# Start of a gated-recurrence and maxout kernel: half masks, GpSimd work moved to VectorE, unit products, a new order of steps

## The chip, the cores and the metric

The kernel runs on one core of a Trainium2 chip. The metric is the device time of one execution in microseconds (us). PE is TensorE (matmuls; PEld its weight loads), DVE is VectorE, ACT is ScalarE, POOL is GpSimd, SP the engine whose queue issues all DMAs here.

## The reference

Two parts, one behind the other. First a gated recurrence ("gateloop") over 4 batches, 8 heads, 768 time steps and head size 48. The gate of each step is a complex number whose size is cut to 0.999; the state is a 48x48 matrix for each head:

```python
mag = np.sqrt(a_re * a_re + a_im * a_im)
scale = np.minimum(mag, 0.999) / (mag + 1e-06)
a_re_n, a_im_n = (a_re * scale, a_im * scale)
for t in range(S):
    new_re = ar * S_re - ai * S_im          # ar, ai: the gate at t, along the rows of the state
    new_im = ar * S_im + ai * S_re
    S_re, S_im = (new_re + outer(k[t], v[t]), new_im)
    y[t] = q[t] @ S_re
```

Then a maxout feed-forward layer over the 3072 tokens, with 384 inputs (8 heads x 48) and 768 hidden units:

```python
h = np.maximum(np.maximum(x @ w1, x @ w2), x @ w3)
out = (h @ w_out).astype(np.float32)
```

The four weight matrices come as 64-bit floats; the rest is 32-bit.

## The kernel before

The recurrence is done in chunks. A group g is 128 time steps of two batches; there are twelve groups (6 along time, 2 pairs of batches). The two blocks of a group, one for each batch, are called x and y; a step's name ends in x or y where it works on one block. Groups 0 and 6 start a sequence.

What is done for a group, by the names that the order uses:

- Loads: `Lr` and `Li` (real and imaginary gate), `Lq`, `Lk`, `Lv`.
- Gates, on 128x768 elements for both blocks (in group 0 on 128x384 for one block, with a 0 or 1 behind the name): `sqr` and `sqi` (squares, ACT), `add` (DVE), `lnL`, `expw`, `expe`, `lne`, `relu` (ACT), `Lnop` (DVE: the tile Ln, minus the logarithm of the gate's size), then the gate's angle: `abs`, `addw`, `lnw`, `expL`, `mulai` (the product ai<-ai,L), `mulw`, `stt`, `sign`, `cpai`, `cpar`, `atan`, `carry` (subtracts the angle carried over from the group before, in one row: ai<-ai,carry), `mulr`, `addi`.
- Angles summed along time: `cs` (PE, product with the triangle matrix `upto`), `t`, `nf`, `af`, `sa`, `sb` (sine and cosine, ACT). `Cd` is a DMA that takes the last rows of nf to the next group as its carry.
- Sums of Ln along time: `sums` (PE, products with the matrices `mid` and `rest`), `En`, `Ek`, `Eq` (ACT), and `F` (PE, products with `cuts`), `f0` to `f3` (ACT).
- `mk`, `mq`, `uk`, `uq` turn k and q by their angles (DVE); `tpk`, `tpq` transpose them (PE, 16 products with `ident` each), `Kc` and `Qc` copy the result out of PSUM (ACT); `Q1` to `Q3`, `QB`, `QG`, `KB`, `kEn` scale them (DVE).
- `A` and `B` are the scores (PE), `g0` to `g3` and `b0`, `b1` copy them out under the masks `maskd` and `masko`; `dk` and `h0` to `h3` make the new state; `y` is the output of the recurrence (PE), copied by the step `x` to the tile xT (so `xx` and `xy` for the blocks).
- Feed-forward: `U` and `u` (products with w1 to w3, in the profile `up`, and their maximum, hT), `O` and `o` (product with w_out, in the profile `op`, and its copy), `D` (store). For group 0 they are done by block: `U20x` is the third part of the hidden units with the first matrix for block x. For later groups, both blocks are done at once.
- Weights: twelve blocks i. `WLi` loads one of 768 KB, and `Wai` to `Wfi` turn it from 64 to 32 bits: a and d on ACT, b, c, e and f on DVE.

The order of the work is written out by hand in two strings. `SCHEDULE` holds the start, word by word as step:group. `CYCLE` is then run for g = 2 to 13 (line 765), with offsets, and skips steps of groups that don't exist. Each engine's instructions are bound to this order: the class `Bound` (lines 120 to 134) makes each instruction follow the one before it on its engine, so that all of them carry line 129 in the profile, and they are told apart by their tiles. SP's queue follows the same order, too; an issue that waits for its buffer holds up all those behind it.

Buffers that matter here: PSUM is one pool of four tiles of two banks (`banks`, line 139), taken in turn; the raw weight blocks lie in parts of the weight tiles that aren't filled yet, in a buffer of Q, or in the two buffers of hT (line 305); the gate tiles L, w and e have one buffer each, ar and ai two.

`ident`, `mid`, `rest`, `upto`, `cuts` and the masks are made on POOL, with memsets on DVE or POOL and selects (`affine_select`, in `keep` and `between`), in `constants_early` (line 206) and `constants_late` (line 233, the step `CL`). `mid`, `rest` and `cuts` have the same content in partitions 0 to 63 and 64 to 127, and `constants_early` makes both halves with a loop over `o`. Besides the masks, POOL does the product `mulai` of the groups from 2 on (line 406) and all carries (line 419).

ACT has its functions in two sets of tables; `activation` (line 147) loads a set when the next function isn't in the present one. Exp and Ln are in one set, Arctan and Sin in the other.

Of the kernel before, what the change touches and what calls it, by code (L numbers as in the profile page):

```python
# [17 lines left out]
OP = mybir.AluOpType  # L18
# [1 line left out]


SCHEDULE = """
Lry:0 sqr1:0 Liy:0 sqi1:0 add1:0 lnL1:0 Lrx:0 Lix:0 sqi0:0 sqr0:0 add0:0 expe1:0 WL0:0 expw1:0 lnL0:0 relu1:0
expw0:0 expe0:0 lne1:0 Lnop1:0 WL1:0 lne0:0 WL2:0 relu0:0 Lnop0:0 Wa0:0 Wd0:0 Wb0:0 Wc0:0 abs1:0 addw1:0 WL3:0
abs0:0 Liy:1 addw0:0 We0:0 Wf0:0 sumsx:0 Eqx:0 Fx:0 f0x:0 Fy:0 lnw1:0 lnw0:0 Wa1:0 Wb1:0 expL0:0 mulai0:0
f3x:0 Wc1:0 mulw0:0 Lqx:0 Wd1:0 We1:0 WL4:0 expL1:0 mulw1:0 Ekx:0 Lrx:1 Wa2:0 sign0:0 stt0:0 Enx:0 f0y:0 Wf1:0
Wb2:0 Wc2:0 cpai0:0 Wd2:0 mulai1:0 We2:0 Wf2:0 f2x:0 cpar0:0 atan0:0 stt1:0 mulr0:0 addi0:0 csx:0 Lkx:0 Wa3:0
Lry:1 Lix:1 atan1:0 sign1:0 Wd3:0 cpai1:0 Lqy:0 tx:0 mqx:0 cpar1:0 WL5:0 Wa4:0 Wb3:0 Wc3:0 We3:0 nfx:0 afx:0
Lvx:0 Wf3:0 mulr1:0 Wb4:0 addi1:0 csy:0 Liy:2 Wc4:0 CL:0 Wd4:0 mkx:0 sax:0 We4:0 sbx:0 ukx:0 f1y:0 uqx:0 f1x:0
tpqx:0 WL6:0 sqr:1 sqi:1 Wf4:0 ty:0 Lky:0 add:1 f2y:0 nfy:0 Qcx:0 Q1x:0 f3y:0 QBx:0 Q2x:0 lnL:1 WL7:0 Wa5:0  # L30
expe:1 Wb5:0 expw:1 Lqy:1 tpkx:0 kEnx:0 Kcx:0 lne:1 relu:1 sumsy:0 QGx:0 Q3x:0 Wc5:0 Lnop:1 Wd5:0 We5:0 Wa6:0
Wb6:0 Ax:0 g0x:0 Wc6:0 abs:1 Eky:0 addw:1 Cdy:0 g1x:0 KBx:0 dkx:0 Cdx:0 mky:0 Eny:0 g2x:0 sign:1 Eqy:0 mqy:0
Wd6:0 We6:0 afy:0 lnw:1 h1x:0 h2x:0 sumsy:1 Eqy:1 mqy:1 expL:1 Wd7:0 Lrx:2 Eny:1 Lry:2 sqr:2 mulw:1 mulai:1
say:0 Wf5:0 sby:0 Wa7:0 g3x:0 stt:1 Wf6:0 cpai:1 uky:0 Bx:0 b1x:0 Wb7:0 h3x:0 Lix:2 Wc7:0 b0x:0 uqy:0 atan:1
carry:1 cpar:1 WL8:0 We7:0 sqi:2 add:2 mulr:1 yx:0 xx:0 Eky:1 Wd8:0 Wf7:0 Lvy:0 addi:1 tpqy:0 Qcy:0 Q2y:0
QGy:0 lnL:2 Q1y:0 Wa8:0 Wb8:0 Q3y:0 U20x:0 U10x:0 u20x:0 u10x:0 tpky:0 Kcy:0 KBy:0 csy:1 expe:2 ty:1 nfy:1
Lky:1 csx:1 expw:2 tx:1 relu:2 kEny:0 Wc8:0 lne:2 U11x:0 WL9:0 Wa9:0 Wd9:0 nfx:1 We8:0 u11x:0 U01x:0 Wf8:0
Wb9:0 Lnop:2 dky:0 h1y:0 h2y:0 U00x:0 Ay:0 g0y:0 u00x:0 sby:1 WL10:0 u01x:0 afy:1 Lkx:1 mky:1 Wc9:0 WL11:0
abs:2 h3y:0 say:1 g1y:0 sign:2 addw:2 lnw:2 U21x:0 u21x:0 g2y:0 We9:0 Cdx:1 Wa10:0 QBy:0 U22x:0 u22x:0 g3y:0
uky:1 expL:2 sumsx:1 Eqx:1 Wf9:0 Enx:1 By:0 b0y:0 b1y:0 Wb10:0 Ekx:1 mulw:2 Fx:1 f1x:1 Lqx:1 mqx:1 Wd10:0  # L40
f3x:1 Wc10:0 f0x:1 mulai:2 stt:2 We10:0 U12x:0 u12x:0 Cdy:1 yy:0 xy:0 Lvy:2 uqy:1 Wf10:0 U02x:0 u02x:0 mkx:1
f2x:1 afx:1 cpai:2 carry:2 atan:2 cpar:2 U20y:0 h0x:1 sax:1 U21y:0 mulr:2 U10y:0 sbx:1 Lkx:2 ukx:1 Lqx:2 Lvx:1
u20y:0 u21y:0 U00y:0 U11y:0 uqx:1 Wa11:0 Wb11:0 U12y:0 u10y:0 u11y:0 Wc11:0 addi:2 tpqx:1 Wd11:0 We11:0 u00y:0
u12y:0 Qcx:1 Q2x:1 QBx:1 tpqy:1 Qcy:1 Lqy:2 U01y:0 u01y:0 Lix:3 csy:2 ty:2 nfy:2 csx:2 tx:2 nfx:2 sbx:2 Wf11:0
Lky:2 QGx:1 U22y:0 tpkx:1 u22y:0 Q1x:1 afx:2 sax:2 Kcx:1 KBx:1 Q3x:1 kEnx:1 tpky:1 U02y:0 Liy:3 u02y:0 Fy:1
f0y:1 f3y:1 f1y:1 f2y:1 Q1y:1 Q2y:1 kEny:1 POx:0 Lrx:3 Kcy:1 sumsx:2 Ekx:2 mkx:2 Enx:2 h0y:1 Eqx:2 Ax:1 g0x:1
Q3y:1 dkx:1 g1x:1 h1x:1 Pox:0 g2x:1 h2x:1 sby:2 g3x:1 h3x:1 afy:2 say:2 Lry:3 sqr:3 Bx:1 QBy:1 b0x:1 sqi:3
ukx:2 POy:0 Ay:1 b1x:1 add:3 g0y:1 g1y:1 lnL:3 KBy:1 Lvx:2 g2y:1 g3y:1 Poy:0 Lvy:1 yx:1 xx:1 PDy:0 Fx:2 f0x:2
dky:1 By:1 sumsy:2 f2x:2 QGy:1 h1y:1 h2y:1 f3x:2 f1x:2 b0y:1 b1y:1 yy:1 expe:3 Eny:2 Eqy:2 xy:1 PDx:0 mqx:2
h3y:1 tpkx:2 Cdx:2 uqx:2 tpqx:2 Eky:2 mky:2 uky:2  # L50
"""
# [12 lines left out]


@with_exitstack
def kernel(
# [15 lines left out]
    P = 128  # L83
# [120 lines left out]
    KB = const.tile([P, 2 * H, 32], FP, name="KB")  # L204

    def constants_early():
        for o in (0, L64):
            halves = mid[o:o + L64].rearrange("p (n u h) -> p n u h", u=2, h=4)
            left, right = halves[:, :, 0], halves[:, :, 1]
            dve.memset(left, -1.0)  # L210
            keep(left, -1, [[-8, 8], [-1, 4]], 1)
            keep(left, 3, [[8, 8], [0, 4]], -1)
            keep(right, -4, [[-8, 8], [0, 4]], 1)
            keep(right, 4, [[8, 8], [1, 4]], -1)
            keep(rest[o:o + L64].rearrange("p (n h) -> p n h", h=8), -4, [[-8, 8], [0, 8]], 1)
        keep(upto, 0, [[1, P]], -1)
        make_identity(nc, ident)
        for o in (0, L64):
            def col(base, n):
                return cuts[o:o + L64, base:base + n]  # L220

            between(col(C8, 4), 7, 11, [[16, 4]], [[16, 4]])
            vw = col(C16, 8).rearrange("p (a v b) -> p a v b", a=2, v=2)
            between(vw[:, :, 0], 3, 19, [[32, 2], [0, 2]], [[32, 2], [8, 2]])
            between(vw[:, :, 1], 15, 19, [[32, 2], [-4, 2]], [[32, 2], [8, 2]])
            vw = col(CB, 6).rearrange("p (a n) -> p a n", a=2)
            between(vw[:, :, 0:2], 3, 7, [[32, 2], [16, 2]], [[32, 2], [16, 2]])
# [137 lines left out]
    def gates(g, cs, name):  # L365
# [37 lines left out]
        elif name == "expL":  # L403
            activation(out=L, in_=L, func=AF.Exp, scale=-1.0)
        elif name == "mulai":
            (pool if g > 1 else dve).tensor_tensor(out=ai, in0=ai, in1=L, op=OP.mult)
        elif name == "mulw":
            dve.tensor_tensor(out=w, in0=w, in1=L, op=OP.mult)
        elif name == "stt":
            dve.scalar_tensor_tensor(out=w, in0=w, scalar=2.0, in1=ai, op0=OP.subtract, op1=OP.mult)  # L410
        elif name == "sign":
            activation(out=ar, in_=ar, func=AF.Sign, bias=tiny)
        elif name == "cpai":
            activation(out=ai, in_=ar, func=AF.Copy, scale=-0.25, bias=0.25)
        elif name == "cpar":
            activation(out=ar, in_=ar, func=AF.Copy, scale=-1.0 / math.pi)
        elif name == "carry":
            if g % NS > 0:
                pool.tensor_tensor(out=ai[0:1], in0=ai[0:1], in1=T["carry", g], op=OP.subtract)
        elif name == "atan":  # L420
            activation(out=w, in_=w, func=AF.Arctan)
        elif name == "mulr":
            dve.tensor_tensor(out=w, in0=w, in1=ar, op=OP.mult)
        else:
            dve.tensor_tensor(out=w, in0=w, in1=ai, op=OP.add)
# [291 lines left out]
    def run(name, g):  # L717

        if g >= NG or g == 0 and name in ("Ox", "ox", "Dx", "Oy", "oy", "Dy"):
            return  # L720
        if name[0] == "P":
            name = name[1:]
        if name == "CL":
# [73 lines left out]
```

## Time and profile before

| what | value |
|---|---|
| three runs, median (lowest to highest) | 645.2 us (644.43 to 646.07) |
| the profiled execution | 646.76 us |
| its span | 645.1 us |
| granted TensorE clock, mean | 0.98 |
| PE, PEld busy | 579.1, 473.3 us |
| DVE, ACT, POOL busy | 475.6, 410.3, 75.2 us |
| POOL products ai<-ai,L: 10, mean | 2.43 us |
| POOL carries ai<-ai,carry: 10, mean | 2.84 us |
| ACT table loads: 30, mean | 1.28 us |
| bytes moved | 39.25 MB |

The page of the profile gives for each engine the time in which it had an instruction under way. The table's rows are sums over the span; how busy an engine was in one stage is read from windows. Two instructions on one engine overlap a little, so the time from start to start of two neighbours is up to 0.1 us under the duration of one. "1.71 <-POOL ai L129" behind an instruction says that its engine stood idle for 1.71 us and that POOL's writing of ai released it.

### The profile page before, as it was taken

What the parts mean: (1) busy time and instruction counts of PE and PEld (TensorE: products, weight loads), DVE (VectorE), ACT (ScalarE), POOL (GpSimd) and SP (SyncE); (2) the same over time, 40 slices, a digit from 0 to 9 for tenths busy, and PEclk for the clock granted to TensorE, in tenths of its full rate; (3) what the DMA queues carried; (4) which work ended last, traced back from release to release, by engine and by line L of the source; (5) the groups of instructions that cost most, each with busy time, mean ns of one, the idle gap of its engine ahead of it and who ended that gap; (6) DMA issues with size and microseconds to landing.
All of it is one profiled execution on the core that took longest, in us unless ns stands there. A gap on an engine that the chain in (4) does not pass through costs nothing.

```text
span 645.1 us, 22666 instructions
## 1 busy us (share of the span) xinstructions
PE 579.1 (90%) x10076; PEld 473.3 (73%) x10076; DVE 475.6 (74%) x680; ACT 410.3 (64%) x676; POOL 75.2 (12%) x91
## 2 busy tenths in 40 slices
PE   1134988998999999999999999999999999999997
PEld 0124877677777777878788788788878778778785
DVE  4799989959778778878668678868859759755111
ACT  7799996777477477486586685774774774530100
POOL 8501040003003002001003003002011011000000
PEclk9997889988999999999999999999999999999999
DMA  9856324342132132132231240250240120000000
GB/s 267 173 136 148 82 73 84 75 87 42 30 68 57 33 67 54 37 66 50 40 74 40 40 85 29 40 100 14 43 97 15 36 56 14 15 14 3 13 13 24
DMA packets 136545, 39.25 MB, mean 61 GB/s; under 512 B 129152, under 2 KB 132224, under 8 KB 136448
## 3 DMA queue, kind: packets, MB, share of 16 engines
q1 hardware_dynamic: 136448, 37.80, 26.8%
q8 instruction: 79, 1.29, 0.9%
q14 instruction: 18, 0.15, 0.1%
HBM read 33.03 MB, written 4.72 MB: 59 GB/s over the span
## 4 chain that ended last, share of the span: by engine, by line
PE 82%; issue 8%; POOL 4%; ACT 2%; DMA 1%; DVE 1%; SPq 1%; POOLq 0%; ACTq 0%; DVEq 0%
PE up L129 42%; PE op L129 15%; PE y L129 6%; PE A L129 4%; PE tp L129 4%; PE dk L129 3%; PE sums L129 2%; PE cs L129 2%; PE B L129 2%; PE F L129 1%; POOL cuts L129 1%; DMA raw<-in_moe_w_dram 1%; POOL ai L129 1%; SPq L129 1%; POOL maskf L129 1%
## 5 line engine op out<-in xcount | busy, mean ns | idle before, releaser
L129 PE MATMUL up<-xT,w 128*128 128x256 f32 (+1 forms) x1404 | 298.3, 370 | 2.2 <-DVE hT L129 1.0
L129 PEld LDWEIGHTS up<-xT,w 128*128 128x128 f32 x1404 | 250.7, 193 | 35.0 <-DVE hT L129 1.2
L129 PE MATMUL op<-wo,hT 128*128 128x384 f32 x288 | 98.8, 494 | 0.0
L129 DVE TENSOR_TENSOR hT<-hT,up 128x768 f32<-128x768 f32 (+1 forms) x56 | 46.8, 836 | 52.7 <-PE up L129 52.7
L129 DVE TENSOR_TENSOR Q<-Q,f 112x512 f32<-112x512 f32 (+2 forms) x72 | 75.9, 1067 | 4.9 <-ACT Q L129 4.2
L129 PEld LDWEIGHTS op<-wo,hT 128*128 128x128 f32 x288 | 53.0, 190 | 33.1
L129 POOL TENSOR_TENSOR ai<-ai,L 128x768 f32<-128x768 f32 x10 | 24.3, 2428 | 389.6 <-ACT L L129 334.4
L129 ACT ACTIVATE f<-F 48x280 f32<-48x280 f32 x96 | 38.1, 398 | 18.5 <-PE F L129 12.9
L129 ACT ACTIVATE t<-cs 128x384 f32<-128x384 f32 x24 | 11.8, 491 | 59.5 <-PE cs L129 59.5
L129 PE MATMUL y<-atm,vb 128*32 128x64 f32 x1152 | 40.6, 228 | 8.4 <-DVE ex L129 8.3
L129 PEld LDWEIGHTS y<-atm,vb 128*32 128x32 f32 x1152 | 33.9, 114 | 17.7 <-issue 17.4
L129 PE MATMUL y<-QG,g 112*32 112x64 f32 x1408 | 39.4, 223 | 0.0
L129 ACT ACT_TABLE_LOAD x30 | 38.5, 1283 | 1.2 <-PEq L781 0.8
L129 ACT COPY ot<-op 128x384 f32<-128x384 f32 x24 | 11.5, 480 | 43.5 <-PE op L129 36.0
L129 DVE SCALAR_TENSOR_TENSOR Ln<-L,e 128x768 f32<-128x768 f32 (+1 forms) x13 | 11.7, 897 | 37.2 <-ACT e L129 36.5
L129 PE MATMUL A<-Q,K 112*32 112x80 f32 x1536 | 32.9, 238 | 5.8 <-DVE Q L129 3.9
L129 POOL TENSOR_TENSOR ai<-ai,carry 1x768 f32<-1x768 f32 x10 | 28.4, 2837 | 70.9 <-ACT ai L129 70.9
L129 PEld LDWEIGHTS A<-Q,K 112*32 112x32 f32 x1536 | 28.5, 112 | 11.0 <-ACT e L129 7.4
L129 PEld LDWEIGHTS y<-QG,g 112*32 112x32 f32 x1408 | 36.1, 112 | 0.0
L129 ACT COPY atm<-B 32x256 f32<-32x256 f32 x48 | 17.3, 361 | 28.5 <-DVE atm L129 25.8
L129 ACT COPY hT<-up 128x768 f32<-128x768 f32 (+1 forms) x28 | 19.8, 708 | 23.1 <-PE up L129 20.7
L129 DVE COPY_PREDICATED atm<-maskd,A 128x512 f32<-128x512 uint8 x24 | 17.6, 734 | 22.0 <-PE A L129 22.0
(96 smaller groups left out, 932.1 us busy)
## 6 DMA issues: line engine op xcount, KB each, us to landing
ar<-in_a_re_dram SPq DMA_DIRECT2D x24, 192.0 KB
ai<-in_a_im_dram SPq DMA_DIRECT2D x24, 192.0 KB
q<-in_q_dram SPq DMA_DIRECT2D x96, 48.0 KB
k<-in_k_dram SPq DMA_DIRECT2D x96, 48.0 KB
vb<-in_v_dram SPq DMA_DIRECT2D x96, 48.0 KB
out_dram<-ot SPq DMA_DIRECT2D x24, 192.0 KB
raw<-in_moe_w_dram SPq DMA_DIRECT2D x5, 768.0 KB
w<-in_moe_w_dram SPq DMA_DIRECT2D x2, 768.0 KB
```

What stands on the lines that cost most here:

```text
L129: ins = f(*a, **kw)
```

## The change

- **Half masks.** `constants_early` makes `mid`, `rest` and `cuts` for partitions 0 to 63 only, and copies each to partitions 64 to 127 on POOL. The order on POOL is now mid and rest, cuts, the memsets of fs, upto, ident, the memsets of vbs; before, the memsets of vbs and fs stood first. `constants_early` is called ahead of the DVE memsets of gs and us. ident is made by two instructions in place of a library call.
- **Products and carries.** `mulai` and `carry` are on DVE for every group.
- **Unit products.** `banks` takes a number from `HOT` for four steps of group 0 and issues that many products of ident with ident (128x128) to the PSUM tile that the step then overwrites: 40 ahead of cs, 23 ahead of tpq, 13 ahead of A, 21 ahead of B, all of block x.
- **Order.** `SCHEDULE` is new, 618 words in place of 472, and reaches one group further: `CYCLE` now starts with g = 3. `CYCLE` has its 143 steps in another order. In it, tables are loaded four times a group; before, twice.

```diff
 def banks(nm, n=None):
     ps = psum.tile([P, 2, 512], FP, tag="ps", name=nm)
+    for i in range(T.pop("hot", 0)):
+        mm(out=ps[:, 0, 0:P], lhsT=ident, rhs=ident, start=True, stop=True)
...
 def constants_early():
-    for o in (0, L64):
-        halves = mid[o:o + L64].rearrange("p (n u h) -> p n u h", u=2, h=4)
...
-    keep(upto, 0, [[1, P]], -1)
-    make_identity(nc, ident)
-    for o in (0, L64):
-        def col(base, n):
-            return cuts[o:o + L64, base:base + n]
...
+    halves = mid[0:L64].rearrange("p (n u h) -> p n u h", u=2, h=4)
...
+    for t in (mid, rest):
+        pool.tensor_copy(out=t[L64:P], in_=t[0:L64])
+
+    def col(base, n):
+        return cuts[0:L64, base:base + n]
...
+    pool.tensor_copy(out=cuts[L64:P], in_=cuts[0:L64])
+    for t in fs:
+        pool.memset(t[L64 // 2:L64], 0.0)
+    keep(upto, 0, [[1, P]], -1)
+    pool.memset(ident, 0.0)
+    pool.affine_select(out=ident, in_=ident, compare_op=OP.not_equal, fill=1.0, base=0, pattern=[[-1, P]],
+                       channel_multiplier=1)
+    for t in vbs:
+        pool.memset(t, 0.0)
...
-    (pool if g > 1 else dve).tensor_tensor(out=ai, in0=ai, in1=L, op=OP.mult)
+    dve.tensor_tensor(out=ai, in0=ai, in1=L, op=OP.mult)
...
-    pool.tensor_tensor(out=ai[0:1], in0=ai[0:1], in1=T["carry", g], op=OP.subtract)
+    dve.tensor_tensor(out=ai[0:1], in0=ai[0:1], in1=T["carry", g], op=OP.subtract)
...
+HOT = {("csx", 0): 40, ("tpqx", 0): 23, ("Ax", 0): 13, ("Bx", 0): 21}
...
+    if (name, g) in HOT:
+        T["hot"] = HOT[name, g]
...
-for g in range(2, NG + 2):
+for g in range(3, NG + 2):
     program(CYCLE, g)
```

The first words of `SCHEDULE`, to the second block's cs:

```diff
-Lry:0 sqr1:0 Liy:0 sqi1:0 add1:0 lnL1:0 Lrx:0 Lix:0 sqi0:0 sqr0:0 add0:0 expe1:0 WL0:0 expw1:0 lnL0:0 relu1:0
-expw0:0 expe0:0 lne1:0 Lnop1:0 WL1:0 lne0:0 WL2:0 relu0:0 Lnop0:0 Wa0:0 Wd0:0 Wb0:0 Wc0:0 abs1:0 addw1:0 WL3:0
-abs0:0 Liy:1 addw0:0 We0:0 Wf0:0 sumsx:0 Eqx:0 Fx:0 f0x:0 Fy:0 lnw1:0 lnw0:0 Wa1:0 Wb1:0 expL0:0 mulai0:0
-f3x:0 Wc1:0 mulw0:0 Lqx:0 Wd1:0 We1:0 WL4:0 expL1:0 mulw1:0 Ekx:0 Lrx:1 Wa2:0 sign0:0 stt0:0 Enx:0 f0y:0 Wf1:0
-Wb2:0 Wc2:0 cpai0:0 Wd2:0 mulai1:0 We2:0 Wf2:0 f2x:0 cpar0:0 atan0:0 stt1:0 mulr0:0 addi0:0 csx:0 Lkx:0 Wa3:0
-Lry:1 Lix:1 atan1:0 sign1:0 Wd3:0 cpai1:0 Lqy:0 tx:0 mqx:0 cpar1:0 WL5:0 Wa4:0 Wb3:0 Wc3:0 We3:0 nfx:0 afx:0
-Lvx:0 Wf3:0 mulr1:0 Wb4:0 addi1:0 csy:0 Liy:2 Wc4:0 CL:0 Wd4:0 mkx:0 sax:0 We4:0 sbx:0 ukx:0 f1y:0 uqx:0 f1x:0
...
+Lrx:0 sqr0:0 Lix:0 sqi0:0 add0:0 WL0:0 lnL0:0 Wa0:0 Wb0:0 Wd0:0 Wc0:0 We0:0 Wf0:0 expe0:0 WL1:0 expw0:0 Wa1:0
+Wb1:0 Wc1:0 relu0:0 lne0:0 Lnop0:0 sumsx:0 Wd1:0 We1:0 WL7:0 Wa7:0 Wb7:0 Wd7:0 Fx:0 Wf1:0 Lry:0 sqr1:0 abs0:0
+f2x:0 addw0:0 Liy:0 sqi1:0 Wc7:0 add1:0 We7:0 WL2:0 sign0:0 Lix:1 Wa2:0 Wb2:0 Lqx:0 WL8:0 Wc2:0 lnL1:0 Lvx:0
+Wd2:0 Wf7:0 lnw0:0 Lqy:0 WL3:0 Lkx:0 expe1:0 expw1:0 lne1:0 We2:0 Wf2:0 relu1:0 Lnop1:0 expL0:0 mulw0:0
+mulai0:0 Wa8:0 Wb8:0 f0x:0 abs1:0 Wd8:0 addw1:0 Wc8:0 stt0:0 Eqx:0 mqx:0 We8:0 Ekx:0 lnw1:0 cpai0:0 expL1:0
+mulw1:0 mkx:0 cpar0:0 mulai1:0 stt1:0 atan0:0 mulr0:0 WL5:0 sign1:0 addi0:0 csx:0 WL6:0 Wf8:0 Lky:0 Lry:1
+Liy:1 atan1:0 cpai1:0 Lvx:1 Wa5:0 Wb5:0 cpar1:0 mulr1:0 CL:0 Lrx:1 WL4:0 Lry:2 tx:0 nfx:0 Wc5:0 Wa6:0 Wb6:0
+afx:0 sbx:0 addi1:0 sax:0 Wc6:0 ukx:0 Wd5:0 We5:0 Wd6:0 We6:0 Enx:0 sqr:1 uqx:0 Wf6:0 f1x:0 tpqx:0 sqi:1 f3x:0
+Wf5:0 tpkx:0 csy:0 add:1 kEnx:0 dkx:0 Qcx:0 Q2x:0 QGx:0 Q1x:0 QBx:0 Kcx:0 Fy:0 lnL:1 KBx:0 Q3x:0 Wa4:0 Wb4:0
...
```

The loop after:

```
CYCLE = """
U00:-1 Kcy:0 Q1x:0 Lry:2 Q2x:0 QBx:0 expe:1 Dy:-2 Q3x:0 Kcx:0 Lix:2 Ax:0 KBx:0 Bx:0 Fy:0 kEny:0 g0x:0 u00:-1
f0y:0 relu:1 Ox:-2 lne:1 g1x:0 g2x:0 g3x:0 b1x:0 Lnop:1 abs:1 addw:1 b0x:0 kEnx:0 f2y:0 f3y:0 f1y:0 Q2y:0
lnw:1 expL:1 U10:-1 mulw:1 u10:-1 mulai:1 ox:-2 sumsx:1 Ekx:1 QGx:0 sign:1 Enx:1 Lkx:1 mkx:1 Eqx:1 Cdx:0 stt:1
dkx:0 Q1y:0 Cdy:0 Lqy:1 atan:1 cpai:1 sumsy:1 U11:-1 h0x:0 h1x:0 Eny:1 h2x:0 Q3y:0 h3x:0 cpar:1 u11:-1 sqr:2
mulr:1 Lqx:1 sqi:2 mqx:1 carry:1 U01:-1 addi:1 Eky:1 Lvy:0 mky:1 KBy:0 Eqy:1 u01:-1 QBy:0 U02:-1 u02:-1 Lrx:3
yx:0 csy:1 xx:0 csx:1 Lvx:1 Ay:0 ty:1 nfy:1 g0y:0 g1y:0 g2y:0 tx:1 afy:1 say:1 nfx:1 sby:1 By:0 g3y:0 U12:-1
b0y:0 add:2 Liy:3 sbx:1 b1y:0 afx:1 mqy:1 sax:1 u12:-1 Fx:1 f1x:1 f2x:1 lnL:2 expw:2 uky:1 dky:0 Oy:-1 h0y:0
oy:-1 Lky:2 QGy:0 f0x:1 h1y:0 h2y:0 f3x:1 Dx:-2 uqx:1 h3y:0 yy:0 tpqx:1 xy:0 uqy:1 tpqy:1 Qcx:1 Qcy:1 ukx:1
tpky:1 tpkx:1
"""
```

## The prediction

> **What bounds the kernel now.** I read the kernel by stages first: busy time of each engine in seven windows (us of the window, then busy us of PE, PEld, DVE, ACT, POOL, granted clock, DMA share, GB/s).
>
> ```profile
> 0.00:16.00 16.00, 1.65 (x18) 1.28 (x18) 7.72 (x28) 11.70 (x21) 14.11 (x48) 1.00 0.97 268
> 16.00:32.00 16.00, 2.34 (x68) 2.04 (x70) 11.55 (x19) 12.63 (x23) 8.40 (x24) 1.00 0.84 175
> 32.00:64.00 32.00, 13.16 (x283) 10.10 (x283) 31.25 (x48) 31.46 (x50) 1.94 (x1) 0.88 0.55 136
> 64.00:113.00 49.00, 44.27 (x714) 40.35 (x704) 47.13 (x71) 41.60 (x65) 7.36 (x3) 0.90 0.35 83
> 113.00:185.00 72.00, 66.69 (x1503) 53.89 (x1501) 59.23 (x85) 48.44 (x84) 4.86 (x2) 0.95 0.29 56
> 185.00:577.00 392.00, 387.81 (x6898) 315.93 (x6893) 300.07 (x411) 258.83 (x426) 38.48 (x15) 1.00 0.23 48
> 577.00:645.00 68.00, 63.13 (x617) 49.70 (x615) 18.62 (x24) 5.67 (x11) 0.00 (x0) 0.99 0.05 16
> ```
>
> PE is busy 579.1 us and idle 66.0. The idle time by window: 28.0 before 32 us, 18.8 to 64, 4.7 to 113, 5.3 to 185, 4.2 to 577, 4.9 in the tail. So from 185 us on PE sets the pace and almost nothing can be won. Ahead of that, from 32 to 113 us, DVE is busy 78.4 of 81 us: the start is bound by DVE's queue. Before 32 us DVE is idle 12.7 of 32 us. What PE waits for:
>
> ```profile
> PE sums L129 <- POOL cuts L129: 12.7, 1, 12.7
> PE cs L129 <- DVE w L129: 11.4, 1, 11.4
> PE y L129 <- DVE ex L129: 8.3, 1, 8.3
> ...
> PE cs L129 <- ACT CS L129: 3.9, 1, 3.9
> PE F L129 <- POOL cuts L129: 3.9, 1, 3.9
> PE A L129 <- DVE Q L129: 3.9, 1, 3.9
> ```
>
> All of these lie before 64 us. The timeline of POOL and DVE shows what the moved products and carries cost (start, duration):
>
> ```profile
> 87.44 5.10 POOL L129 TENSOR_TENSOR ai<-ai,L 128x768 f32<-128x768 f32 x1 [22.99 <-ACT L L129]
> 94.49 1.80 POOL L129 TENSOR_TENSOR ai<-ai,carry 1x768 f32<-1x768 f32 x1 [1.95 <-ACT ai L129]
> ```
> ```profile
> 92.58 0.96 DVE L129 SCALAR_TENSOR_TENSOR w<-w,ai 128x768 f32<-128x768 f32 x1 [1.71 <-POOL ai L129]
> ...
> 94.66 2.46 DVE L129 TENSOR_TENSOR uq<-CS,q 128x768 f32<-128x768 f32 x1
> ```
>
> POOL takes 5.10 us for a product that DVE does in 0.96, DVE waits 1.71 us for it, and a DVE step beside the carry takes 2.46 us where its group's mean is 1.02.
>
> [...] the first eight cs products took 1.55 us, sixteen later ones 1.45.
>
> **The change, part by part.** I price queues by start-to-start times of before: DVE 0.87 us for a 128x768 step, 0.47 for 128x384, ACT 0.75 and 0.41, a table load 1.28. On PE at full clock: an up of 18 matmuls 4.0, op 4.07, y 1.72, A 1.25, and so on for all; over the whole kernel this gives 567 us, so of PE's 579 some 12 is slow clock. Added along each engine's order, in us, before / after:
>
> - ahead of the first cs (group 0, block x): DVE 14.7 / 20.2, ACT 20.5 / 23.0
> - ahead of the first y: DVE 50.0 / 51.3, ACT 55.2 / 53.0, PE 8.4 / 8.7
> - ahead of the first op of group 0: DVE 95.4 / 95.2, ACT 96.6 / 94.8, PE 48.5 / 51.5
> - through the last y of group 2: DVE 141.7 / 149.0, PE 110.6 / 111.7
>
> *Masks.* 21 of the 42 selects on mid, rest and cuts go (0.26 to 0.29 us each), three copies come (a 64x64 cast took 0.23). POOL starts about 1.5 us, since the memset of mid now stands ahead of those of g: five selects and two copies to 3.3, sixteen selects and a copy to about 8.3 (before: 18.2), f 1.06, upto 0.67, ident 0.8, the four vb memsets 2.76, to 13.6. F's 3.9 us wait goes. What is late next is DVE's w for cs, so this alone moves nothing on the end. The v load now waits for vb at 13.6; SP stands behind earlier loads until about then, so I cost it at nothing (if not, the q and k loads behind it slip by a few us).
>
> *Order to the first cs.* The new order does block x first and puts weight blocks 0, 1 and 7 between the gates. A block is one load of 0.79 MB, 2.9 us at the 268 GB/s of the first window, two steps on ACT (0.81, 0.83) and four on DVE (0.47, 0.48, 0.87, 0.87). Loads come in SP's order, at that rate from about 2.2 us: block 0 at 6.6, block 1 at 9.5, block 7 at 12.5, y's two inputs at 13.9, block 2 at 16.9, block 8 at 21 to 23 (q and ai between), k of x at 26 to 28. Walking ACT and DVE beside them, each step at the later of its queue and its input: ln's table ends at 6.7; block 0 is on DVE to 10.8; Ln of x is ready at 12.3 (before: both halves at 12.6); block 1 to 14.7; block 7 to 19.6, with y's inputs ahead of it on DVE; block 2 to 21.4; the second Ln 21.9; x's two products 22.4 and 22.8; block 8 waits for its load, to 26.1; the table for atan 26.3 to 27.6; addi 29.1. With small loads slower than the rate, 30.5. So cs starts near 30 against 31.16, but DVE has by then done 20.2 instead of 14.7: it lags its queue sum by 9 to 10 us instead of 16.4. That is 6.5 us won for DVE, all from its 12.7 idle us before 32.
>
> *From there to the first op.* Before: 112.2 us, so the lag of DVE's sum was 16.8, the same as at cs. After: 95.2 + 9.5 = 104.7 from DVE. But PE has 42.8 us of full-clock work between the first y (51.3 + 9.5 = 60.8) and that op, and lost 8.9 of 49 us in that window before (4.7 idle, 4.2 slow clock). I let it keep half: 60.8 + 42.8 + 5 = 109. PE's lag (time less PE's sum) is then 57.5 against 112.2 - 48.5 = 63.7: 6.2 us won.
>
> *Products and carries.* Ten of each leave POOL (2.43 and 2.84 us); DVE gets 0.87 for each (the 1x768 has the same elements in a row, so the same price; a floor of 0.4 and a ceiling of 0.96). Per group 1.7 us more on DVE, less the stretches seen (1.14 at 152, 1.6 at 158, 1.5 at 94): near nothing. In the loop DVE is 77% busy, so that hides it; in the start the queue sums above have it in. If the cover were gone it is 0.3 us a group.
>
> *Unit products.* 97 of 128x128: twelve up matmuls of that shape took 1.53 us, 0.127 each, twice that cold: 5 to 10 us ahead of cs, 3 to 6 of tpqx, 2 to 3 of A, 3 to 5 of B. Cover: F ends about 15.5 and cs starts at 30; between cs and tpqx DVE has 8.5 us of queue; A and B each have about 6. All hidden; uncovered, the two last would cost up to 4. I give them no gain of their own.
>
> *113 to 185 us.* Before lost 5.3 idle and about 4 slow. In the new order DVE's sum plus 14 (the lag when PE is at 109) leaves it 5 us ahead of PE through group 2's last y (163 against 170), and PE has no cold start; 4.5 of the 9 goes.
>
> *The loop.* Same PE work. ACT gets four table loads a group instead of two: 2.57 us more, at 66% busy. I cost it at nothing. SP: the carry DMAs now stand behind steps that finished long ago (before, SP stood 19.0 us for nf at one); the early ar load for group 2 stands for a buffer that frees about 33 us, with loads of groups 1 and 2 behind it that are not yet due.
>
> Sum: 6.2 + 4.5 = 10.7 us. The profiled execution was 646.8 with a span of 645.1, so about 636 for it; the median of before, 645.2, is 1.6 under it, so 634.5 for the median.
>
> **Rivals.** *Hidden anyway:* PE was already 90% busy from 64 us, so DVE's lead may end in PE's queue. Then only the masks and F count, and 644.5 comes out. Against: DVE waits little and PE's waits to 64 us name DVE. *More:* PE stays warm and the start loses nothing: 4.5 more and 4 of the slow clock, 626. *Slower, by the loop:* A of a group follows one up (4.0) on PE and needs K's copy. On ACT, after the last y, stand xT's copy, two Q copies, a K copy, an exp and the second K copy: 0.48 + 3 x 0.92 + 0.75 + 0.92 [...], about 5.3; PE has four tp (2.1) and the up, 6.1. The margin is 0.85 us. If the extra tables make ACT late by their 2.57, PE waits 1.7 in each of nine loops, 15.5: 645.2 - 10.7 + 15.5 = 650. It decides from 1.2 us a loop on. Against: ACT is a third idle.
>
> **Numbers.** Forecast 0.56 (634.5, own range 629 to 641); more 0.12; hidden 0.15, of which a part is still faster; slower 0.17. A change of 0.3%, 1.9 us, is what a measurement can tell. Faster 0.71, same 0.12, slower 0.17. The range runs from 626 (cs at 27 us, nothing lost later) to 648, which takes in the hidden case and the slower end's first third.
>
> **What would show it.** Right: cs about 30 us with DVE busy over 22 us before it; the first op near 109; PE idle under 61 us and slow clock gone after 64; no DVE step of 384 or 768 over 1.1 us beside POOL; from 185 us on the same idle. Wrong: the first op at 112 or later; a wait of A or cs for ACT that comes back in each group; cs waiting behind unit products.

## The result

After: 643.83 us (median of 12 runs, 640.95 to 646.12). Before, on the same chip: 645.13 us (12 runs, 643.49 to 646.66). Ratio 0.9979, 95% interval 0.9961 to 0.9997: 1.3 us faster, where 10.7 were forecast. The two profiled executions lie at the ends of their groups, 646.76 before and 640.95 after, with granted clocks of 0.980 and 0.989; they show 5.8 us where the medians show 1.3. So moments of single profiles are read below to about 2 us (e1 and e9 below are the same program up to the first op, and their profiles have it at 108.9 and 111.1), and worths from ratios of many runs.

The profile after, by the same stages (columns as before):

```profile
0.00:16.00 16.00, 0.00 (x0) 0.00 (x0) 9.86 (x25) 9.63 (x14) 9.87 (x37) 1.00 0.93 261
16.00:32.00 16.00, 12.45 (x128) 12.01 (x128) 15.41 (x27) 15.24 (x29) 4.34 (x3) 0.97 0.86 223
32.00:64.00 32.00, 24.11 (x370) 22.03 (x370) 27.41 (x43) 28.63 (x47) 6.04 (x13) 0.85 0.63 135
64.00:113.00 49.00, 43.68 (x854) 39.86 (x857) 47.85 (x73) 43.76 (x72) 0.00 (x0) 0.97 0.28 67
113.00:185.00 72.00, 65.75 (x1470) 53.84 (x1459) 61.45 (x92) 50.90 (x83) 0.00 (x0) 1.00 0.33 66
185.00:577.00 392.00, 388.28 (x6899) 315.81 (x6898) 305.18 (x427) 275.88 (x438) 0.00 (x0) 1.00 0.22 47
```

DVE is idle 6.7 us before 32 where it was idle 12.7: fed earlier, as forecast. But from 32 to 64 it is idle 4.6 us where it had been idle 0.75, and from 113 to 185 PE is still idle 6.3 (5.3 before). PE's larger busy time before 64 is unit products, 27 us of it. The waits up to 185 us (total, times, longest):

```profile
PE sums L138 <- DVE Ln L138: 16.4, 1, 16.4
DVE atm L138 <- PE A L138: 4.6, 2, 4.4
PE cs L138 <- DVE w L138: 4.1, 1, 4.1
PE A L138 <- DVE nf L138: 3.9, 1, 3.9
```

F no longer waits for the cuts. New is VectorE's wait for A, 4.4 us. The first Ln came at 15.7 and the first cs at 32.97, not at 12.3 and 30; the first op at 114.0, not at 109. Two rows of the timeline (start, duration) show the first of these:

```profile
8.75 3.85 DVE L138 TENSOR_SCALAR ex<-ex 128x768 f32<-128x768 f32 x2 [2.61 <-ACT ex L138]
...
9.41 2.78 POOL L138 MEMSET vb<- 128x768 f32 x4
```

Two weight steps took 3.85 us beside GpSimd's memsets of vb; the same pair took 1.15 at 14.61: 2.7 us lost, about as long as the four memsets (2.78). With the memsets in the same place other profiles lost less (the pair took 2.48 in e2, 2.54 in e14, 1.70 in e9, 1.17 in e1), and with the memsets first nothing (1.16 in e3). Why such a step takes longer beside memsets on GpSimd no run here shows.

The second failing place:

```profile
50.97 4.80 PE L138 MATMUL A<-ident 128*128 128x128 f32 x26 [3.90 <-DVE nf L138]
...
55.70 1.31 PE L138 MATMUL A<-Q,K 112*32 112x80 f32 x64
...
57.15 0.73 DVE L138 COPY_PREDICATED atm<-maskd,A 128x512 f32<-128x512 uint8 x1 [4.36 <-PE A L138]
```

The 13 unit products ahead of A (two instructions each) write A's PSUM buffer, so they start only when that buffer is free, at 50.97, and A itself starts 4.7 us later. They are in A's way, not in an idle stretch.

### The profile page after: what moved, and what is told of

Its sections match the earlier page's. It is cut to its first block, busy times and chain, and to the rows that moved or that the text cites. A ratio compares the mean times of both kernels' runs of the same rounds, so it can differ in the third digit from the quotient of the medians.

```text
span 639.2 us, 22955 instructions
## 1 busy us (share of the span) xinstructions
PE 592.0 (93%) x10270; PEld 489.2 (77%) x10270; DVE 480.1 (75%) x699; ACT 429.1 (67%) x690; POOL 20.2 (3%) x53
## 4 chain that ended last, share of the span: by engine, by line
PE 85%; DVE 8%; ACT 3%; issue 3%; DMA 1%; SPq 0%; DVEq 0%; ACTq 0%
PE up L138 44%; PE op L138 15%; PE y L138 6%; PE A L138 5%; PE tp L138 4%; PE dk L138 3%; PE sums L138 3%; DVE ex L138 2%; PE cs L138 2%; DVE w L138 2%; PE F L138 2%; PE B L138 2%; DMA w<-in_moe_w_dram 1%; DVE Q L138 1%; ACT CS L138 0%
## 5 line engine op out<-in xcount | busy, mean ns | idle before, releaser
L138 PE MATMUL up<-xT,w 128*128 128x256 f32 (+1 forms) x1404 | 292.5, 366 | 3.3 <-ACT xT L138 2.7
L138 PEld LDWEIGHTS up<-xT,w 128*128 128x128 f32 x1404 | 248.0, 190 | 39.9 <-ACT xT L138 3.2
L138 DVE TENSOR_TENSOR hT<-hT,up 128x768 f32<-128x768 f32 (+1 forms) x56 | 46.6, 834 | 48.6 <-PE up L138 48.5
L138 DVE TENSOR_TENSOR Q<-Q,f 112x512 f32<-112x512 f32 (+2 forms) x72 | 67.7, 951 | 11.3 <-ACT Q L138 9.7
L138 ACT COPY xT<-y 128x384 f32<-128x384 f32 x24 | 11.5, 479 | 65.6 <-PE y L138 65.6
L138 ACT COPY hT<-up 128x768 f32<-128x768 f32 (+1 forms) x28 | 19.8, 708 | 36.1 <-PE up L138 36.1
L138 PEld LDWEIGHTS y<-atm,vb 128*32 128x32 f32 x1152 | 32.4, 111 | 11.6 <-issue 8.2
L138 PE MATMUL y<-atm,vb 128*32 128x64 f32 x1152 | 39.3, 223 | 1.0 <-issue 0.8
L138 PEld LDWEIGHTS y<-QG,g 112*32 112x32 f32 x1408 | 34.9, 110 | 2.0 <-ACT g L138 1.0
L138 DVE COPY_PREDICATED atm<-masko,A 128x256 f32<-128x256 uint8 x72 | 31.2, 433 | 1.6
L138 PE MATMUL sums<-Ln,mid 64*64 64x192 f32 x192 | 14.1, 351 | 16.4 <-DVE Ln L138 16.4
L138 PE MATMUL dk<-vb,uk 64*48 64x48 f32 (+1 forms) x1408 | 24.9, 215 | 3.2 <-issue 1.6
L138 DVE TENSOR_TENSOR QG<-Q,f 112x1024 f32<-112x1024 f32 (+1 forms) x24 | 27.1, 1129 | 0.9 <-PE y L138 0.9
```

What stands on the lines that cost most here:

```text
L138: ins = f(*a, **kw)
```

## The experiments

Every run is compared with before on its own chip. Starts are of the profiled execution (us); "PE's lag" is the first op's start less PE's queue sum ahead of it (48.5 in the old order, 51.5 in the new), the prediction's own measure of PE's progress. It also holds what the granted clock cost in that execution: from 64 to 113 us the clock was 0.90 in before, 0.93 in e13, 0.94 in e7 and 1.00 in e1, e5 and e6.

| run | first cs | first A | first op | PE's lag | median | ratio to before (95%) |
|---|---|---|---|---|---|---|
| before | 31.2 | 47.8 | 112.2 | 63.7 | 645.1 | 1 |
| after | 33.0 | 55.7 | 114.0 | 62.5 | 643.83 | 0.9979 (0.9961 to 0.9997) |
| e1, no unit products | 30.8 | 49.5 | 108.9 | 57.4 | 642.30 | 0.9949 (0.9934 to 0.9965) |
| e2, none ahead of A | 32.3 | 51.8 | 115.9 | 64.4 | 645.13 | 0.9992 (0.9969 to 1.0015) |
| e3, memsets first | 30.3 | 54.9 | 113.2 | 61.7 | 643.09 | 0.9971 (0.9950 to 0.9991) |
| e4, e2 and e3 | 32.0 | 50.5 | 115.7 | 64.2 | 643.98 | 0.9975 (0.9959 to 0.9992) |
| e5, e1 and e3 | 31.9 | 51.4 | 111.2 | 59.7 | 642.26 | 0.9953 (0.9938 to 0.9968) |
| e6, e1 in the old order | 27.3 | 43.9 | 106.4 | 57.9 | 639.74 | 0.9908 (0.9877 to 0.9940) |
| e7, products and carries alone | 31.2 | 47.9 | 110.4 | 61.9 | 643.26 | 0.9971 (0.9955 to 0.9986) |
| e8, order alone | 34.9 | 54.4 | 114.5 | 63.0 | 646.77 | 1.0026 (1.0006 to 1.0046) |
| e9, e1 with one op moved | 31.8 | 50.3 | 111.1 | 59.6 | 644.99 | 0.9972 (0.9952 to 0.9991) |
| e11, e7 with two steps of F later | 28.1 | 45.2 | 107.7 | 59.2 | 640.47 | 0.9914 (0.9895 to 0.9933) |
| e12, e6 with unit products | 27.3 | 48.4 | 111.0 | 62.5 | 642.09 | 0.9938 (0.9924 to 0.9951) |
| e13, half masks alone | 27.2 | 43.8 | 108.6 | 60.1 | 642.68 | 0.9942 (0.9923 to 0.9961) |
| e14, units ahead of cs and tpq only | 31.4 | 50.4 | 110.2 | 58.7 | 644.56 | 0.9970 (0.9955 to 0.9985) |

**The two failing places (e1 to e5).** First theory: the walk was right, and the memsets and the unit products spoil it. Rival: hidden anyway.

```diff
e1: -HOT = {("csx", 0): 40, ("tpqx", 0): 23, ("Ax", 0): 13, ("Bx", 0): 21}
    +HOT = {}
e2: +HOT = {("csx", 0): 40, ("tpqx", 0): 23, ("Bx", 0): 21}
e3:  (the loops that clear vb and f on pool stand ahead of constants_early(), not in it)
e4:  e2 and e3      e5: e1 and e3
```

e1: 

> The changed kernel without any unit product. Theory 1 (the 13 unit products ahead of A, which could only start at 50.97 us when their PSUM buffer came free and took 4.7 us, hold up A, and DVE with it for 4.4 us; those of cs, tpq and B are hidden): A starts as soon as the buffer is free, runs cold at about 2.4 us instead of 1.3, so DVE wins about 3.5 us and loses up to 1 us to cold cs and tpq: 640 to 642 us against 643.8. Theory 2 (the unit products pay by keeping the clock up between 32 and 136 us): 646 us or more, with a lower granted clock in those windows. Theory 3 (PE's own queue hides what DVE wins): 643.8 within 1 us.

e2: 

> The changed kernel without the unit products of A alone. Theory 1: as the run without any, but tpq stays warm: 640 to 641 us, DVE's wait for A about 1 us in place of 4.4. Theory 2: at most 1 us faster or slower than the changed kernel, since a cold A gives back what is won. Theory 3: 643.8 within 1 us.

e3: 

> The changed kernel with the memsets of the v and f tiles on GpSimd ahead of the masks, as before the change. Theory 1 (a GpSimd memset beside a VectorE tensor_scalar holds the latter: the first two took 3.85 us instead of 1.15): these two take about 1.2 us, the first Ln comes about 13 us and cs about 30.5 instead of 33, and 2 to 2.5 us come through to the end: 641.5 us. Rival (the stretch is due to something else, such as the DMA traffic): the two still take over 3 us and the time stays at 643.8. Theory 3 (hidden later): the steps are short again and cs is early, but the end stays at 643.8 within 1 us.

e4: 

> Both edits: memsets first and no unit products ahead of A. Theory 1: the two gains add, 638 to 639 us, the first op at about 107 to 108 us instead of 114. Theory 3: 643 or more.

e5: 

> The kernel after with no unit products and with GpSimd's memsets of the vb and f buffers ahead of its masks instead of behind them. Theory (the prediction's first step, the walk of group 0 on VectorE, was right and was spoilt by two of the change's own parts): the first Ln ends before 13.8 us, the first cs starts near 30, A near 49, the first op near 108, as in the run with no unit products, and the median lands at 641.5 to 642.5, because that run already had its op at 108.9. Rival (the two repairs add up at the end, 3.0 us for the unit products and 0.7 for the memsets): 641.0 or less, with the first op at 107 or earlier. Rival (neither repair is worth anything, the differences seen so far are the spread of the runs): 644 to 645.

With no unit products the first op comes at 108.9 in e1, where the walk had put it, but at 111.2 in e5 and 111.1 in e9. By the ratios e1 is about 1.9 us faster than after, with intervals that just touch. With the memsets first the cs came at 30.3 (e3), but e5, with both repairs, is no faster than e1, and its cs is at 31.9: that repair's worth at the end isn't shown. Leaving out A's set alone (e2, and e4 with the memsets first) gave nothing back. A starts earlier (51.8 where it was 55.7), but then B's set takes 7.40 us in place of 4.96 and ends no earlier. (A itself took 2.36 us in before, without unit products, and 1.31 in after, behind them.) First after, then e2:

```profile
56.94 4.96 PE L138 MATMUL B<-ident 128*128 128x128 f32 x42
```

```profile
55.20 7.40 PE L138 MATMUL B<-ident 128*128 128x128 f32 x42 [1.05 <-ACT E L138]
```

So the theory explains where the walk broke, and not where its 10.7 us are: even e1, with its walk as forecast, gains 3.

**Taking the change apart (e6, e7, e8, e13).** New theory: the order is the gain. Rival: the masks and products are.

```diff
e6:  after with SCHEDULE and CYCLE of before, the loop from 2, HOT = {}
e7:  before with
     -(pool if g > 1 else dve).tensor_tensor(out=ai, in0=ai, in1=L, op=OP.mult)
     +dve.tensor_tensor(out=ai, in0=ai, in1=L, op=OP.mult)
     -pool.tensor_tensor(out=ai[0:1], in0=ai[0:1], in1=T["carry", g], op=OP.subtract)
     +dve.tensor_tensor(out=ai[0:1], in0=ai[0:1], in1=T["carry", g], op=OP.subtract)
e8:  before with SCHEDULE and CYCLE of after, the loop from 3
e13: before with constants_early of after, called first, and no other clearing of vb and f
```

e6: 

> The kernel after with the order of the kernel before (both lists and the first turn of the loop), and no unit products: half masks, and products and carries on VectorE, alone. Theory (the order written out by hand for the first three groups is what shortens the walk; masks and products only let it): the first cs stays at 31 to 32, the first op at 111 to 113, and the median within 1 us of before, 644.5 to 646. Rival (the masks and the products did it, the order nothing): the first op at 109 to 110 and 642.3, as the run with the new order and no unit products.

e7: 

> The kernel before with one edit: its products of ai and L and its carries on VectorE instead of GpSimd. The prediction put this part near nothing: VectorE gets 10 products of 0.9 us and 10 carries of 0.8 us more, beside TensorE, and the steps beside them are no longer stretched. Theory: within 0.7 us of before. Rival 1 (GpSimd's products hold VectorE back and this does cost): 1.5 to 3 us faster. Rival 2 (17 us more of VectorE's work in the loop is not all hidden): 1 to 3 us slower.

e8: 

> The kernel before with one edit: the lists of the kernel after (order of the first three groups and of the loop). Masks are still built twice on GpSimd (the cuts are ready at 18.3 us, as before), the products of the third group on and the carries stay on GpSimd; no unit products. Theory (the order does it): the first Ln ends at 12.5 to 13.5, F waits for the cuts until 18.4 but TensorE has nothing else to do then, the first cs at 30 to 31, the first op at 109 to 111 (one or two VectorE steps are stretched by GpSimd's products), and 642.5 to 643.5. Rival (the order needs the masks and the products off GpSimd): the first op at 112 or later and 644.5 or more.

e13: 

> The kernel before with one part of the change alone: the half masks, built once and copied, with the memsets of vb and f behind them on GpSimd as in the change. Products and carries stay on GpSimd, the order is that of before, no unit products. Theory (masks, products, order and unit products each have their own worth, which adds up; the masks' is that ScalarE no longer stands at F): the first cs at 27.3 to 28, the first op near 108.3 (4.0 before the 112.2 of before), 3 to 4.5 us faster than before, 641 to 642. Rival (the prediction's step: the masks alone move nothing on the end, because VectorE's w is late next): the first cs at 31 and within 1 us of before. Rival (masks and products are worth their sum only together): 1.5 to 2.5 us faster.

The theory fell, three times over. The old order with the new masks and products has the lowest ratio of all (0.9908); the order alone is slower than before; and the masks alone bring the first cs from 31.2 to 27.2 and 3.8 us to the end. The parts add up: masks 0.9942 and products 0.9971 give 0.9913, against 0.9908 measured. What the masks do is in the profile of before, in rows that the prediction didn't use. Its waits up to 34 us:

```profile
DVE ex L129 <- ACT ex L129: 4.6, 2, 4.3
ACT f L129 <- POOL maskf L129: 4.4, 1, 4.4
PE F L129 <- POOL cuts L129: 3.9, 1, 3.9
```

and its timeline of ScalarE and VectorE there:

```profile
14.33 0.49 ACT L129 ACTIVATE E<-sums 128x384 f32<-128x384 f32 x1
19.25 0.40 ACT L129 ACTIVATE f<-F 48x280 f32<-48x280 f32 x1 [4.43 <-POOL maskf L129]
...
20.37 0.87 ACT L129 ACTIVATE ex<-w 128x768 f32<-128x768 f32 x1
...
21.27 0.58 DVE L129 TENSOR_SCALAR ex<-ex 128x768 f32<-128x768 f32 x1 [4.35 <-ACT ex L129]
```

ScalarE takes its steps in order. It stands 4.43 us at the exponential of F, and behind it stand the gate's Ln and the weight step that VectorE needs: so VectorE stands 4.35 us too. (The releaser is put down to `maskf`, but F itself waited for the cuts to 18.3.) In e13 the two waits are 0.2 us each:

```profile
DVE ex L129 <- ACT ex L129: 0.4, 2, 0.2
...
ACT f L129 <- PE F L129: 0.2, 1, 0.2
```

The products and carries act at the start, too. From the first cs of group 0 to that of group 1 it is 40.8 us in before and 38.8 in e7 (41.2 in e13 and 39.4 in e6, the same pair with half masks). First before, then e7:

```profile
63.15 1.73 DVE L129 TENSOR_SCALAR ex<-ex 128x768 int32<-128x768 int32 x1
...
65.89 1.10 PE L129 MATMUL tp<-ident,uq 64*112 64x64 f32 x16 [0.69 <-DVE uq L129]
66.92 4.52 PE L129 MATMUL up<-xT,w 128*128 128x128 f32 x24
```

```profile
63.23 0.55 DVE L129 TENSOR_SCALAR ex<-ex 128x768 int32<-128x768 int32 x1
...
66.28 3.04 PE L129 MATMUL up<-xT,w 128*128 128x128 f32 x24
```

Beside group 1's carry (62.06 to 64.46 on GpSimd) a VectorE step takes 1.73 us instead of 0.55. So uq comes 1.1 us later, PE stands 0.69 us for it, and the up behind it runs slowly for longer: the granted clock from 64 to 68 us is 0.50 in before and 0.69 in e7. It is not cs's own wait: the w that cs needs is written only 0.2 us earlier in e7. (The first product on GpSimd comes later, at 87 us.) Whether the clock came up later because of PE's wait no run tests.

**Is it ScalarE's place in line? (e11)** If so, the masks aren't needed for it: moving the step that waits is enough.

```diff
-... Eqx:0 Fx:0 f0x:0 Fy:0 ... mulai0:0 f3x:0 Wc1:0 ... sign0:0 stt0:0 ...
+... Eqx:0 Fx:0 Fy:0 ... mulai0:0 Wc1:0 ... sign0:0 f0x:0 f3x:0 stt0:0 ...
```

> The kernel before with its products and carries on VectorE (643.3) and one more edit: two of ScalarE's exponentials of F for group 0 are moved some 5 us later in the order, behind the sign step. The masks are still built twice on GpSimd and F still waits for the cuts until 18.3 us, as before. Theory (the whole worth of the half masks is that ScalarE, which takes its steps in order, no longer stands 4.4 us at the exponential of F with the weight and gate steps behind it): the first cs near 27.5 instead of 31.2, the first op near 106.5, and 639.5 to 641, as with the half masks. Rival (the half masks are worth their 3.5 us through GpSimd's shorter work beside VectorE, or through F itself): 643 or more.

As the theory said: two words of the order, with the masks built twice as before, take e7's 0.9971 to 0.9914; the half masks take it to 0.9908 (e6). First the row of cs with products and carries moved alone (e7), then with f0x and f3x later as well (e11):

```profile
31.24 1.55 PE L129 MATMUL cs<-w,upto 128*64 128x192 f32 x8 [11.39 <-DVE w L129]
```

```profile
28.10 1.55 PE L129 MATMUL cs<-w,upto 128*64 128x192 f32 x8 [6.28 <-DVE w L129]
```

**The unit products (e12, e14).**

```diff
e12: e6 with the HOT of the change
e14: after with HOT = {("csx", 0): 40, ("tpqx", 0): 23}
```

e12: 

> The kernel after with the lists of before (half masks, products and carries on VectorE, 639.7 without unit products) and with the unit products of the change. Theory (the products ahead of A and B start only when their PSUM buffer comes free, and so stand in the way of A and B; they cost in any order): A starts 2 to 4 us later than the 43.9 of the run without them, the first op at 107.5 or later, and the median at 640.5 to 642. Rival (they cost only where the new order puts them, and warm TensorE here): 639 to 640, first op at 106 or earlier.

e14: 

> The kernel after with its unit products ahead of cs and tpq of group 0 alone: those ahead of A and B are left out. Theory (in the new order the first two sets end before the step behind them is due, and the whole 1.5 us that the unit products cost comes from A's and B's): as the run with none, 2.7 to 4 us faster than before, the first op at 108.5 to 111. Rival (the sets ahead of cs and tpq cost too, as leaving A's alone out had suggested, 0.9992 of before): 0.5 to 2 us faster than before.

In the old order the ratio is 0.9938 with them and 0.9908 without: about 1.9 us again, but with intervals that overlap, so at the end the cost is likely here, not shown. The first op comes 4.6 us later. Here it is tpq's set that is late:

```profile
34.23 7.04 PE L130 MATMUL tp<-ident 128*128 128x128 f32 x46
...
41.20 0.66 PE L130 MATMUL tp<-ident,uq 64*112 64x64 f32 x16
```

Without them tpq started at 36.2: 5.0 us lost, and every set after it starts from there. The set ahead of the first cs costs nothing (27.29 with and 27.30 without in the old order; in after PE still waits 4.15 us behind it). With it that cs takes 0.87 us in e12, where PE waits 1.72 us between them, and 1.55 without it in e6; in after, behind the wait of 4.15, it takes 1.55 all the same. In the new order tpq's set is hidden (in e14 tpq still waits 0.79 us for uq behind it). e14 has its first op 3.8 us ahead of after's, so A's and B's sets together delay that op, and by e2 (115.9) B's alone does as much; but e14's ratio, 0.9970, lies between after's and e1's with intervals that touch both. How the cost at the end divides over the sets stays open.

**Where the new order loses (e9, e10).** With unit products in both, the new order (after, 0.9979) is slower than the old (e12, 0.9938), and the intervals don't touch. Without them it is 0.9949 (e1) against 0.9908 (e6). Up to the first op PE is as far in e1 as in e6 (lag 57.4 and 57.9), in e5 and e9 about 2 us less far. From 113 to 185 us PE is busy 63.9 us in e1, 65.6 in e5 and 67.05 in e6. The lag and the idle time there together are 65.5 in e1, 66.1 in e5 and 62.9 in e6: by 185 us the new order is about 3 us behind. PE's idle rows in e1 from 117 to 136 name no releaser:

```profile
120.21 0.39 PE L138 MATMUL sums<-Ln,mid 64*64 64x192 f32 x3 [0.73 <-issue]
...
124.37 0.69 PE L138 MATMUL B<-QB,KB 112*32 112x32 f32 x31 [1.55 <-issue]
...
128.55 0.22 PE L138 MATMUL y<-atm,vb 128*32 128x64 f32 x1 [1.46 <-issue]
...
132.44 0.38 PE L138 MATMUL F<-cuts,Ln 64*48 64x35 f32 x16 [1.42 <-issue]
```

They come every 3.9 to 4.2 us and in the middle of a step (B's second instruction), and between two of them lie 127 or 128 matmuls and as many weight loads each time. Theory: PE gets its instructions in portions of 256, and a stretch of small matmuls runs faster than they arrive. The new order puts group 0's two ops (24 matmuls in 8 us) back to back and then nothing but small products. e10 asks for that rate alone; e9 moves one op into the stretch.

```diff
e10: -mm(out=ps[:, 0, 0:P], lhsT=ident, rhs=ident, start=True, stop=True)
     +mm(out=ps[32 * (i % 4):32 * (i % 4) + 32, 0, 0:64], lhsT=ident[:, 0:32], rhs=ident[:, 0:64], start=True, stop=True)
     on e6, with HOT = {("U00", 11): 700}
e9:  -POy:0 ... POx:0 ... Q2y:1 ... KBx:1 ... yx:1 xx:1 KBy:1 ...
     +POy:0 ... Q2y:1 ... KBx:1 ... yx:1 xx:1 POx:0 KBy:1 ...   (Pox:0 behind b0y:1)
```

e10: 

> The kernel after in the old order without the change's unit products, and ahead of the last group's first up 700 extra products, 32 columns of weights by 64 elements with 128 rows, into a PSUM buffer that the up then overwrites: only TensorE's rate for small matmuls is asked. They have no wait between them, the other engines have little to do, and the DMAs carry almost nothing. Theory (instructions arrive at 256 in about 4.1 us): after the first few hundred the products come in blocks of 128, each block with its weight loads takes about 4.1 us, with a gap of 1 to 2 us between them, so 700 take 20 to 23 us. Rival (no such limit; the gaps seen were waits): 0.02 us each as in the fastest stretches, 14 to 15 us, without recurring gaps.

e9: 

> The run with no unit products, with one step moved: of the two ops of group 0, which stand back to back in the new order (8.0 us of large matmuls from 108.9), the second goes behind the y of group 1's first block, into the stretch of small matmuls from 117 to 136 us. Theory (TensorE's instructions arrive no faster than 256 in 4.1 us, so a stretch of small matmuls without a large one in it runs at that rate; this is where the new order loses the lead that it has at the first op): the gaps of about 1.5 us that recur every 128 matmuls there fall from four to two or fewer, TensorE's idle time from 109 to 185 falls from 8.1 us to 6 or less, and the median from 642.3 to 640 to 641.3. Rival (the gaps are waits for VectorE or for buffers that the trace doesn't name): the gaps stay or move, 642 to 643.5.

```profile
600.70 1.99 PE L130 MATMUL up<-ident 128*32 128x64 f32 x128 [1.23 <-issue]
604.45 1.99 PE L130 MATMUL up<-ident 128*32 128x64 f32 x128 [1.75 <-issue]
...
637.61 1.10 PE L130 MATMUL up<-ident 128*32 128x64 f32 x63 [1.75 <-issue]
```

The limit is shown: products that wait for nothing, in the otherwise idle tail, come in blocks of 128, mostly 1.99 us busy and about 1.7 idle. From 600.70 to 637.61 are ten blocks, 3.69 us each. The queue that brings the instructions shows the same portions (packets, MB, share of the DMA engines' time; first e10, then e6):

```profile
q8 instruction: 90, 1.47, 0.9%
```

```profile
q8 instruction: 79, 1.29, 0.8%
```

Eleven packets more go with 2800 more instructions, 1400 matmuls and as many weight loads: one packet for 256. Between 600 and 637 us there are ten, one for each block. (Each product is two instructions, so 700 gave 1400 and took 40 us; the expectation had counted one. The rate, a block's time, is what it asked for, and it is nearer 3.7 than 4.1.) As a cause of e1's loss at the end it is not shown: in e9 the four gaps became two (1.75 us at 122.13 and 0.92 at 135.92), but B and dk now stood behind the moved op (ScalarE waited 5.2 us for B, VectorE 5.6 for dk), PE was idle 7.4 us from 113 to 185 instead of 8.1, and e9 is not faster than e1. That the new order falls behind by about 3 us before 185 is seen in two profiles, e1's and e5's. How much of it is the arrival of instructions and how much the new neighbours of each wait stays open; nor did a run part the order of the start from that of the loop.

## Why the prediction was wrong, step by step

The forecast booked its whole 10.7 us on the order, 6.2 up to the first op and 4.5 behind it, and nothing on the other three parts. At the end of the kernel, in us:

| part | forecast | measured |
|---|---|---|
| masks | 0 | 3.8 faster (e13) |
| products and carries | near 0 | 1.9 faster (e7) |
| order | 10.7 faster | 1.7 slower (e8) to 2.6 slower (e6 to e1) |
| unit products | 0 | about 1.9 slower (e1 to after) |

So the step that failed most is the gain of the order. The prediction counted VectorE's 12.7 idle us before 32 as time that the new order fills. But 4.35 us of them were the stall at F, which the masks alone end (e13). With the masks and the products the old order has about the same lag at the first op (57.9 in e6) as the new one (57.4, 59.7 and 59.6 in e1, e5 and e9). The 4.5 us behind the first op didn't come. Why the new order ends up slower stays open. Step by step:

- *Masks: "What is late next is DVE's w for cs, so this alone moves nothing on the end."* This step failed, and it hid what the order was then credited with. The prediction followed F's wait on PE, where nothing urgent stood behind it, and not on ScalarE, where everything did. "DVE's w", which it named as late next, was late because of that very wait.
- *Order to the first cs: near 30 with 20.2 us of DVE's queue done.* Right as a walk: 30.75 in e1 and 31.76 in e9, which is the same program up to there (32.97 in after, where the memsets delay it). Wrong as a gain. VectorE's lag fell from 16.4 to 10.5, but 4 us of the 16.4 was the stall at F, gone with the masks: the old order then has cs at 27.3. The new order does 5.5 us more of VectorE's work ahead of it and starts cs 3.4 us later. (The small loads did come slower: in before 165 GB/s from 20 to 24 us, where 3523 of 3524 packets are under 512 bytes, against 268 in the first 16.)
- *First op: 109, 6.2 us of PE's lag won.* The number came in e1 (108.9, lag 57.4, 6.3 won), but that profile was a lucky one: 4.0 and 4.1 won in e5 and e9. Its source was another: masks 3.6 (63.7 to 60.1 in e13) and products 1.8 (61.9 in e7).
- *vb's memsets: not priced against VectorE.* 2.7 us ahead of the first Ln in after, less in other profiles; the prediction asked only who waits for vb.
- *Products and carries: "near nothing".* A VectorE step is stretched beside GpSimd, as it said (1.73 us where e7 has 0.55); why, no run shows. On VectorE a product of 128x768 takes 0.95 us and a carry of 1x768 takes 0.94 (after), near the 0.87 that it booked for each. The size at the end was not near nothing: 0.9971, 1.9 us. The prediction weighed the stretches at 94, 152 and 158 us against VectorE's extra work and left out the one at 63 us, the step that PE's next work waits for.
- *Unit products: "All hidden; uncovered, the two last would cost up to 4."* They weren't hidden, and they were priced at half: the 0.127 us of a matmul in the profile is one instruction, and a product of ident is two. A's 13 took 4.80 us, not 2 to 3, and tpq's 23 took 7.07, not 3 to 6. "Twice that cold" shows in the trace of after: the matmuls of tpq's set start 0.22 us apart at a granted clock of 0.50 (36.1 to 37.4) and 0.11 apart at 1.00 (39.8 to 41.1). They start when their PSUM buffer comes free, which for A is when A is nearly due.
- *113 to 185: 4.5 us won.* Nothing was: PE's idle time there is 5.3 before, 6.3 after, 8.1 in e1, 5.0 in e6. The granted clock did rise there, from 0.95 to 1.00, but it is 1.00 in e6 and e7, too, in the old order. VectorE's sums put it ahead of PE, and by the trace PE's longer gaps there don't wait for it: they name no releaser.
- *The loop at nothing.* Right: PE's idle time from 185 to 577 is 3.7 us after and was 4.2, with four table loads a group. The slower rival's wait of A in each group didn't come. (The ScalarE steps that it lists add up to 4.9 us against PE's 6.1; its margin of 0.85 was the author's estimate.)

In ratios: masks -0.6%, products -0.3%, order about +0.4% (e6 to e1), unit products +0.3% (e1 to after); the sum, -0.2%, is the measured change. (The last two are steps of one chain of runs that ends in after, so the sum tests nothing of its own; e6 tests that masks and products add up.) The rival "hidden anyway" (644.5) came nearest, for a reason that was mostly not its own: two parts of the change gave back what two others won. Of e1's lead at the first op half is gone at the end, but in gaps of PE, not in its queue. The fastest kernel found, e6, is the change without its order and its unit products: 639.74.

## What to carry to other kernels

When a wait goes away, look at what is queued behind it on each engine that takes part in it, in order, before saying what is late next: here a wait of PE that cost nothing was a wait of ScalarE that cost 4 us, and moving two words cured it as well as rebuilding the masks did. Extra products that are to shorten the step behind them belong into a buffer that is free long before that step, and have to end before it is due, or they stand in its way: here A came 4.7 us after its buffer was free. Price each part of a large change by taking it out alone: the parts here had both signs, and their sum hid that.

## What the runs showed of the hardware

- In a long run of small matmuls that wait for nothing, PE got through 256 instructions (128 matmuls and as many weight loads) in 3.69 us on average (e10, ten blocks from 600.70): 128 matmuls of 128x32 by 64 were mostly done in 1.99 us and then PE waited about 1.7. Ten packets of the instruction queue came in that time, one for each block. The kernel's loop, with 1571 matmuls and weight loads in 40 us (e6, 300 to 340), about 145 in 3.69, stays below this rate on average.
- Four GpSimd memsets of 128x768 (2.78 us) held a pair of VectorE `tensor_scalar` steps of 128x768 for 2.7 us in after (3.85 against 1.15) and for 1.3 in e2 (2.48), where the memsets took 3.18. Beside selects of small masks such a pair took 1.16 to 1.29 (e5). Where the pair ended before the memsets began (e1, 9.59 and 9.68) it took 1.17, and the next one, at 11.60, 1.86.
- A 128x128 product of f32 tiles shows as two matmul instructions (13 as 26, 21 as 42): 13 took 4.80 us behind an idle PE and 21 took 4.96 right after (after), about 0.37 and 0.24 us each.
- Executions of one kernel differ by 5 us and more on one chip, in part with the granted clock (after: 645.4 us at 0.981, 641 to 643.75 at 0.987 to 0.989).
